# Six words of a hand-written order, each one slice further from the words that feed them, in an attention and two-layer mixture-of-experts kernel

## The chip, the cores and the metric

The kernel runs on one core of a Trainium2 chip, as one program of one launch. The metric is device time in microseconds of one execution. The median of three runs before the change is 425.94 us (424.27 to 426.3).

## The reference

Linear attention over 4 batches of 576 tokens and 8 heads of 64, then two mixture-of-experts layers over the 2304 rows of 512 that it gives. Each layer has 8 experts of 512 x 1024 x 512, and a token goes to the one expert with the largest logit.

```python
q_s = softmax(q, over the 64 of a head);  k_s = softmax(k, over the 576 tokens)
kv = np.einsum('bhsd,bhse->bhde', k_s, v)
x = np.einsum('bhsd,bhde->bhse', q_s, kv)        # then reshaped to 2304 x 512

# layer 1: capacity 576 tokens for each expert, counted in order of tokens
logits = x @ w_gate;  expert_idx = argmax(logits);  gate_w = max of softmax(logits)
out[i] = gate_w[i] * (relu(x[i] @ w1[e]) @ w2[e])      # 0 where the expert is full

# layer 2: only tokens with x @ w_skip > 0
out = x + gate_w * (relu(x @ w1b[e]) @ w2b[e])         # else out = x
```

## The kernel before, in words

The tokens lie transposed in memory, 512 features in four pieces of 128 partitions and 576 tokens of a batch in the free dimension. Attention of a batch is done in two halves of four heads (the objects `c` to `i`, class `Half`). Routing of a batch in a layer is a `Route` object: `C0` to `C3` for layer 1, `M0` to `M2` for layer 2. An expert with more than 32 tokens of a batch is a "large" one and is computed for all 576 tokens of the batch at once, with the gate weights set to zero for the tokens of others (class `Group`). An expert with up to 32 tokens is a "small" one: its tokens are gathered first (class `Small`, the objects `S` and `T`).

A group has 16 slices. Slices 0 to 7 are products with the first weights (line 839), slices 8 to 15 with the second (line 860). A slice is 24 matmuls of 288 columns. Each 32-bit operand is split in a high and a low part (lines 781 and 782, on ScalarE and VectorE), and a product is three matmuls: high by high, high by low, low by high. Its result lies in one of two pairs of PSUM banks (`pair`). In slices 0 to 7 ScalarE and VectorE take it out as `hh` and `hl` (lines 873 and 874). The slice after the next writes to the same pair, and so waits for `hl`.

The order of everything after the start is written by hand in the table `COURSE`: five groups of 16 lines each. In line i the program issues the products of slice i, then the split of the weights of slice i + 2 (`split_w`), then the words ahead of the bar, then the evacuation of slice i, then the words behind the bar. Each engine does its own instructions in that order. A word is a step of another piece of work that is placed among the slices. Those that matter here:

- `C0.3`, `M0.3`, `M1.3` (`w3`, line 621): VectorE makes the one-hot table `oh` of the chosen expert, a chain of small instructions that ends in line 632 or, in layer 2, in line 636.
- `C0.4`, `M0.4`, `M1.4` (`w4`, line 638): 17 small TensorE matmuls in 16 bits on `oh` count positions and tokens of each expert in the bank `pp` (lines 644, 652, 660 and 669). VectorE then copies `pos` and `cnt` out (lines 674 to 678).
- `C0.5`, `M0.5`, `M1.5` (`w5`, line 680): VectorE makes the list of large and small experts from `cnt`, some 15 to 20 instructions of one to eight columns.
- `g.rw`, `i.rw` (line 507): for batch 3 the gate weights of layer 1 are multiplied into k v. TensorE turns the product of k and v (`kvd`) in the bank `pkT`, ScalarE copies it as `kT` (line 513), TensorE multiplies with the gate weights (`pkw`, line 517), VectorE copies the result `kw` out (line 520).
- `i.kz` (line 413): VectorE adds k's exponentials over the tokens of a partition in three instructions (lines 417 to 419). `i.kv` then turns these sums on TensorE (line 426) and multiplies k and v (line 437).
- `d.km` (line 374): VectorE takes maxima of k in three instructions (lines 378 to 380). `d.kt` turns them on TensorE (line 386). `c.qt` turns q (lines 463 and 470), `c.qn` and `c.q3` normalise q and take exponentials (lines 362 to 367, and 334).

Of the kernel before, what the change touches and what calls it, by code (L numbers as in the profile page):

```python
# [45 lines left out]
    L4 c.qm | C0.1 c.km  # L46
    c.q1 | c.kt
    L5 c.q2 | C0.2 c.kc
    C0.3 c.ke d.qm | C0.4
    L6 C0.5 c.q3 | c.kv  # L50
    c.qn d.q1 |
    L7 d.km | c.qt d.kt
    C0.6 d.q2 | d.kc
    d.ke | c.re G.0
# [26 lines left out]
    ((0, 2), """  # L81
    L4 C2.5 | M0.1
    C2.6 | M0.2
    L5 G.3 S.p M0.3 | S.g0 M0.4
    M0.5 | S.g1 G.1
    L6 M0.6 S.l | S.g2
    | S.g3 G.2
    L7 | S.g4
# [9 lines left out]
    """),  # L98
    ((1, 0), """
    L4 G.3 | g.rw  # L100
    | M2.1
    L5 | M2.2 M1.1
    M2.3 | M2.4
    L6 M2.5 | G.1
    M2.6 | M1.2
    L7 T.p M1.3 T.l G.2 | T.g0 M1.4
    M1.5 | T.g1
    M1.6 N0 | T.g2
    X0 i.qm | T.g3
    N1 i.km i.q1 | T.g4 i.kt  # L110
    X1 i.q2 | T.gx i.kc
    N2 i.ke | T.t00 O0.0
    X2 i.kz i.q3 | i.kv
    N3 i.qn | T.t01 O0.1
    X3 T.v0 | T.t02 i.qt
    """),
    ((1, 1), """
    L4 G.3 | T.t03 O0.2
    | T.a0 i.rw
    L5 | T.t04 C3.1  # L120
    T.v1 | T.t10 T.u00
    L6 | T.u01 C3.2 G.1
    C3.3 | T.t11 C3.4 O0.3
# [15 lines left out]
def kernel(  # L139
# [18 lines left out]
    B, H, S, D = q.shape  # L158
    DM = out.shape[1]
    E = w_gate.shape[1]  # L160
# [21 lines left out]
    def bank(name):  # L182
        return pa.tile([P, 512], F32, name=name, tag="a")
# [39 lines left out]
    wg = []  # L223
    for i, g in enumerate((w_gate, w_gate2)):
        t = cp.tile([P, NC, 32], F32, name=f"wg{i}")
        nc.gpsimd.memset(t, 0.0)
        with nc.allow_non_contiguous_dma(reason="gate weights are small"):
            nc.scalar.dma_start(out=t[:, :, 0:E], in_=g.rearrange("(c p) e -> p c e", p=P))
            if i == 1:
                nc.scalar.dma_start(  # L230
                    out=t[:, :, E:E + 1], in_=w_skip.rearrange("(c p o) -> p c o", p=P, o=1)
# [33 lines left out]
    class Half:  # L265
# [241 lines left out]
        def rw(self):  # L507

            kT = self.tile([P, 2, P], "kT", "m2")
            pt = bank("pkT")  # L510
            for c in range(2):
                nc.tensor.transpose(pt[:, c * P:(c + 1) * P], self.kd[:, c], ident)
            nc.scalar.copy(kT, pt[:, :2 * P].rearrange("p (c t) -> p c t", c=2))
            pt = bank("pkw")
            o = 2 * self.hh
            for c in range(2):
                nc.tensor.matmul(
                    out=pt[:, c * E:(c + 1) * E], lhsT=kT[:, c], rhs=wg[0][:, o + c, 0:E], start=True, stop=True
                )
            nc.vector.tensor_copy(out=kw[:, o:o + 2, 0:E], in_=pt[:, :2 * E].rearrange("p (c e) -> p c e", c=2))  # L520

# [956 lines left out]
```

## Time and profile before

| | |
|---|---|
| median of three runs | 425.94 us (424.27, 425.94, 426.3) |
| the profiled execution | 423.36 us; span of its instructions 421.5 us |
| TensorE (PE) busy in the span | 396.1 us, 94% |
| weight loads (PEld) | 351.3 us, 83% |
| VectorE (DVE) | 251.8 us, 60% |
| ScalarE (ACT) | 182.5 us, 43% |
| GpSimd (POOL) | 12.3 us, 3% |
| DMA | 54.48 MB, mean 129 GB/s |
| mean granted clock of TensorE | 0.994 |

The profile is of one execution, whose time lies 2.58 us below the median. A matmul of the large groups overlaps with the next, so a row's duration is longer than its distance to the next row. "[1.10 <-DVE oh L636]" behind a row says that the engine stood idle for 1.10 us ahead of it, and what ended that.

### The profile page before, as it was taken

Reading aid. Unit: us, or ns where it says so; the run is one execution under the profiler, and the core shown is the slowest. Engines: PE = TensorE matmul, PEld = TensorE weight load, DVE = VectorE, ACT = ScalarE, POOL = GpSimd, SP = SyncE. Lnnn points to the kernel's source line nnn. Section 1 sums busy time; section 2 is a strip of 40 time slices with the busy share of each in tenths; the row PEclk is TensorE's granted clock in tenths of the full one; section 3 lists DMA queues with packets and bytes.
Section 4 is the critical chain, followed back from the end, with each engine's and each line's share of the span. In section 5 each row is a group of like instructions: output and inputs, shape, how many; then the busy total and the mean of one; then the engine's idle time right before and its main releaser. Section 6 shows DMA issues by size and latency. Waiting matters only on the chain.

```text
span 421.5 us, 8456 instructions
## 1 busy us (share of the span) xinstructions
PE 396.1 (94%) x3241; PEld 351.3 (83%) x3241; DVE 251.8 (60%) x640; ACT 182.5 (43%) x547; POOL 12.3 (3%) x46
## 2 busy tenths in 40 slices
PE   8989879999999999998999999998999999899893
PEld 4656779898999889798999888798998987799882
DVE  3875788463686755378446746367676736554431
ACT  1556666634257771423347523332375333231111
POOL 2400000000000000000000100000000000000000
PEclk9999999999999999999999999999999999999997
DMA  8819935200960300392544861117315555363134
GB/s 199 221 51 255 235 93 163 58 2 2 310 159 25 106 2 2 111 291 68 163 166 151 241 180 51 50 52 231 98 51 180 178 178 174 92 212 145 30 90 110
DMA packets 72536, 54.48 MB, mean 129 GB/s; under 512 B 18455, under 2 KB 67115, under 8 KB 72491
## 3 DMA queue, kind: packets, MB, share of 16 engines
q1 hardware_dynamic: 70536, 53.60, 44.1%
q10 hardware_dynamic: 1954, 0.31, 0.5%
q8 instruction: 26, 0.43, 0.4%
q14 instruction: 20, 0.16, 0.1%
HBM read 49.16 MB, written 4.73 MB: 128 GB/s over the span
## 4 chain that ended last, share of the span: by engine, by line
PE 70%; DVE 6%; ACT 3%; issue 2%; DVEq 0%; ACTq 0%
PE pair L860 29%; PE pair L839 21%; PE pxs L1147 2%; PE pk L437 2%; PE pl L593 2%; PE pto L1281 2%; PE ph L1203 1%; PE py L1203 1%; PE pts L1252 1%; PE px L495 1%; ACT hh L873 1%; PE ptq L463 1%; DVE wl L782 1%; PE ptx L1162 1%; DVE hl L874 1%
## 5 line engine op out<-in xcount | busy, mean ns | idle before, releaser
L860 PE MATMUL pair<-hh,wh 128*128 128x288 f32 x320 | 98.2, 307 | 0.0
L860 PE MATMUL pair<-hh,wl 128*128 128x288 f32 x320 | 94.4, 295 | 0.0
L860 PE MATMUL pair<-hl,wh 128*128 128x288 f32 x320 | 94.4, 295 | 0.0
L839 PE MATMUL pair<-xh,wh 128*128 128x288 f32 x304 | 92.9, 305 | 0.0
L839 PE MATMUL pair<-xl,wh 128*128 128x288 f32 x304 | 89.6, 295 | 0.0
L839 PE MATMUL pair<-xh,wl 128*128 128x288 f32 x304 | 89.4, 294 | 0.0
L782 DVE TENSOR_TENSOR wl<-ws,wh 128x512 fp32r<-128x512 f32 x80 | 54.9, 686 | 36.4 <-ACT wh L781 34.8
L873 ACT ACTIVATE hh<-pair 128x576 fp32r<-128x576 f32 x40 | 25.9, 647 | 88.6 <-PE pair L839 86.8
L860 PEld LDWEIGHTS pair<-hh,wh 128*128 128x128 f32 x320 | 60.4, 189 | 3.8 <-issue 2.6
L860 PEld LDWEIGHTS pair<-hl,wh 128*128 128x128 f32 x320 | 60.6, 189 | 0.1
L860 PEld LDWEIGHTS pair<-hh,wl 128*128 128x128 f32 x320 | 60.4, 189 | 0.0
L839 PEld LDWEIGHTS pair<-xh,wh 128*128 128x128 f32 x304 | 57.0, 188 | 2.3 <-issue 0.9
L874 DVE SCALAR_TENSOR_TENSOR hl<-pair,hh 128x576 fp32r<-128x576 f32 x40 | 30.2, 756 | 46.4 <-ACT hh L873 46.4
L839 PEld LDWEIGHTS pair<-xl,wh 128*128 128x128 f32 x304 | 57.1, 188 | 0.1
L839 PEld LDWEIGHTS pair<-xh,wl 128*128 128x128 f32 x304 | 57.1, 188 | 0.0
L781 ACT CAST wh<-ws 128x512 fp32r<-128x512 f32 x80 | 49.3, 620 | 2.6 <-DMA ws<-in_moe_w_dram 1.7
L334 ACT ACTIVATE eq<-qt,mx 128x64 f32<-128x64 f32 x140 | 46.7, 338 | 0.3 <-DVE mx L323 0.3
L334 ACT ACTIVATION_READ_ACCUMULATOR eq<-qt,mx 128x1 f32 x140 | 26.6, 190 | 0.0
L532 PE MATMUL pair<-warm 128*128 128x384 f16 x94 | 19.7, 359 | 1.6 <-DVE warm L949 1.6
L782 DVE TENSOR_TENSOR xl<-x,xh 128x576 fp32r<-128x576 f32 x20 | 14.9, 752 | 6.0 <-ACT xh L781 6.0
L1282 ACT COPY ot<-pto 128x256 f32<-128x256 f32 (+1 forms) x24 | 7.0, 316 | 26.0 <-PE pto L1281 26.0
L532 PEld LDWEIGHTS <-warm 128*128 128x128 f16 x94 | 9.6, 107 | 8.8 <-issue 3.2
(210 smaller groups left out, 499.9 us busy)
## 6 DMA issues: line engine op xcount, KB each, us to landing
ws<-in_moe_w_dram SPq DMA_DIRECT2D x39, 512.0 KB, 5.4
tw<-in_moe_w_dram SPq DMA_DIRECT2D x24, 512.0 KB, 4.1
kt<-in_k_dram SPq DMA_DIRECT2D x8, 512.0 KB, 7.7
qt<-in_q_dram SPq DMA_DIRECT2D x8, 512.0 KB, 6.8
out_dram<-ot SPq DMA_DIRECT2D x12, 256.0 KB, 2.7
vt<-in_v_dram SPq DMA_DIRECT2D x16, 128.0 KB, 4.5
vt<-in_v_dram SPq DMA_DIRECT2D x3, 512.0 KB
mg<-gate SPq DMA_DIRECT2D x4, 288.0 KB, 6.1
```

The lines of the kernel that those rows point to most:

```text
L334: nc.scalar.activation(self.eqv[:, h, j], self.qt[:, h, j], AF.Exp, bias=self.mx[:, i:i + 1], accum_out=self.qz[:, i:i + 1])
L437: nc.tensor.matmul(out=pk[64 * g:64 * g + 64, c * D1 + o:c * D1 + o + n], lhsT=self.kt[:rows(j), 2 * c + g, j], rhs=ones32[:rows(j), 0:1] ...
L532: nc.tensor.matmul(out=pw[:, 0, :3 * P], lhsT=warm16[:, 0:P], rhs=warm16, start=True, stop=True)
L593: nc.tensor.matmul(out=pl[32 * c:32 * c + 32, :HT], lhsT=self.weights[:, c], rhs=self.chunk(c, tokens(a)), start=True, stop=True,)
L781: nc.scalar.copy(hi, src)
L782: nc.vector.tensor_tensor(out=lo, in0=src, in1=hi.bitcast(F32), op=ALU.subtract)
L839: nc.tensor.matmul(out=self.pt[:, a, :HT], lhsT=u[:, c], rhs=w[:, c, tokens(a)], start=(c == 0 and n == 0), stop=(c == NC - 1 and n == 2),)
L860: nc.tensor.matmul(out=self.pt[:, a, :HT], lhsT=p_[:, f], rhs=w[:, tokens(a)], start=(v == 0 and f == 0 and n == 0), stop=(v == 1 and f == ...
L873: nc.scalar.activation(halves(hh), src, AF.Relu)
L874: nc.vector.scalar_tensor_tensor(out=halves(hl), in0=src, scalar=0.0, in1=halves(hh).bitcast(F32), op0=ALU.max, op1=ALU.subtract,)
L1147: nc.tensor.matmul(out=self.px[:, c * self.w:(c + 1) * self.w], lhsT=self.xt[:rows(j), c * P:(c + 1) * P], rhs=self.pj[:rows(j), j], start ...
L1203: nc.tensor.matmul(out=self.ph[32 * g:32 * g + 32, :256], lhsT=lhsT, rhs=rhs, start=(i % 4 == 0), stop=(i % 4 == 3))
```

## The change

Six words are moved by one place, and `rw` is cut in two so that its second half can stand apart:

- `C0.4` from behind the bar of slice 3 to ahead of the bar of slice 4 in the first group, `C0.5` from slice 4 to slice 5;
- `M0.4` and `M1.4` in the same way (slices 2 to 3 of the third group, 6 to 7 of the fourth), with `M0.5` and `M1.5` from ahead of the bar to behind it;
- `g.rw` and `i.rw` keep the turn and the copy `kT`; the matmuls `pkw` and the copy `kw` are the new words `g.rx` and `i.rx`, one slice later;
- `i.kz` from ahead of the bar of slice 13 of the fourth group to behind the bar of slice 12.

```diff
-    C0.3 c.ke d.qm | C0.4
-    L6 C0.5 c.q3 | c.kv
-    c.qn d.q1 |
+    C0.3 c.ke d.qm |
+    L6 C0.4 c.q3 | c.kv
+    C0.5 c.qn d.q1 |
...
-    L4 G.3 | g.rw
-    | M2.1
+    g.rx | M2.1
...
-    N2 i.ke | T.t00 O0.0
-    X2 i.kz i.q3 | i.kv
+    N2 i.ke | T.t00 O0.0 i.kz
+    X2 i.q3 | i.kv
...
             nc.scalar.copy(kT, pt[:, :2 * P].rearrange("p (c t) -> p c t", c=2))
+            self.kT = kT
+
+        def rx(self):
             pt = bank("pkw")
```

On VectorE, in slices 3 to 5 of the first group (`hl` is the evacuation of a slice, `wl` the low part of the weights, `pos` and `cnt` belong to C0.4, `keep` begins C0.5), before:

```order
L874 SCALAR_TENSOR_TENSOR hl<-pair_83,hh 128x576
L674 COPY pos<-pp 128x40
L676 TENSOR_TENSOR cnt<-pp,rem 128x8
L782 TENSOR_TENSOR wl_208<-ws_201,wh_204 128x512
L685 TENSOR_TENSOR keep<-pos,rem 128x40
```

and with the change:

```order
L877 SCALAR_TENSOR_TENSOR hl<-pair_83,hh 128x576
L785 TENSOR_TENSOR wl_208<-ws_201,wh_204 128x512
L677 COPY pos<-pp 128x40
L679 TENSOR_TENSOR cnt<-pp,rem 128x8
L877 SCALAR_TENSOR_TENSOR hl<-pair_84,hh 128x576
L454 TENSOR_SCALAR rz<-pk 128x2
L455 RECIPROCAL rz<-rz 128x2
L458 TENSOR_TENSOR kvd_113<-pk,rz 64x2x64 x2
L785 TENSOR_TENSOR wl_209<-ws_201,wh_205 128x512
L688 TENSOR_TENSOR keep<-pos,rem 128x40
```

The two copies now stand behind a split of weights and ahead of the next slice's `hl`, and C0.5 stands behind that `hl` and the four rows that follow it. What stands behind C0.5 (`c.qn`, then an `hl`, a `wl` and `d.km`) keeps its place.

On VectorE, in slices 12 and 13 of the fourth group (`s` is i.kz, `ot` a copy of a store, `xl` the low part of the next group's input), before:

```order
L1282 COPY ot<-pto 128x256
L782 TENSOR_TENSOR wl_209<-ws_201,wh_205 128x512
L782 TENSOR_TENSOR xl<-x_122,xh 128x576
L417 TENSOR_TENSOR s_3878<-kt 128x512
L418 TENSOR_TENSOR s_3879<-s_3878 128x256
L419 TENSOR_TENSOR s_3879<-s_3879,kt 128x256
```

and with the change:

```order
L1285 COPY ot<-pto 128x256
L417 TENSOR_TENSOR s_3850<-kt 128x512
L418 TENSOR_TENSOR s_3851<-s_3850 128x256
L419 TENSOR_TENSOR s_3851<-s_3851,kt 128x256
L785 TENSOR_TENSOR wl_209<-ws_201,wh_205 128x512
L785 TENSOR_TENSOR xl<-x_122,xh 128x576
```

The three sums pass the two splits.

On TensorE, at slices 0 and 1 of the fourth group, before:

```order
L839 MATMUL pair_84<-xh,wl_206 128x288
L512 MATMUL pkT<-c_85,kvd_113 128x128 x2
L517 MATMUL pkw<-wg_93,kT 128x8 x2
L839 MATMUL pair_83<-xh,wh_203 128x288
L839 MATMUL pair_83<-xl,wh_203 128x288
```

and with the change, at the turn and then at the end of slice 1:

```order
L512 MATMUL pkT<-c_85,kvd_113 128x128 x2
L842 MATMUL pair_83<-xh,wh_203 128x288
L842 MATMUL pair_83<-xl,wh_203 128x288
```

```order
L842 MATMUL pair_83<-xh,wl_207 128x288
L520 MATMUL pkw<-wg_93,kT 128x8 x2
L596 MATMUL pl<-x_123,wg_96 32x288 x8
```

The 24 matmuls of slice 1 now stand between `pkT` and `pkw`. The matmuls of `pp` pass the 24 of the next slice in the same way at their three places. No instruction is added or taken away, and the orders of ScalarE, GpSimd and the DMA queue are as before.

## Rows read from the trace of the kernel before

**Rows 1.** Waits of TensorE: engine, line, releaser: us in total, times, longest.
```profile
PE pp L644 <- DVE oh L636: 2.2, 2, 1.1
```
**Rows 2.** Timeline of TensorE around C0.4: start, us, engine, line, operation [idle before].
```profile
58.72 0.27 PE L644 MATMUL pp<-oh,c 128*128 128x32 f16 x4 [2.12 <-DVE oh L632]
...
59.48 0.40 PE L839 MATMUL pair<-xh,wh 128*128 128x288 f32 x1
...
62.87 1.83 PE L437 MATMUL pk<-vt,kt 128*64 128x65 f32 x40
...
72.39 0.38 PE L386 MATMUL pt<-c,m 128*128 128x128 f32 x2
```
**Rows 3.** Timeline of TensorE at M0.4 (third group) and M1.4 (fourth group).
```profile
197.45 0.27 PE L644 MATMUL pp<-oh,c 128*128 128x32 f16 x4 [1.10 <-DVE oh L636]
...
290.42 0.26 PE L644 MATMUL pp<-oh,c 128*128 128x32 f16 x4 [1.13 <-DVE oh L636]
```
**Rows 4.** Timeline of TensorE at g.rw (fourth group) and i.rw (fifth group).
```profile
262.49 0.38 PE L512 MATMUL pkT<-c,kvd 128*128 128x128 f32 x2
263.65 0.61 PE L517 MATMUL pkw<-wg,kT 128*128 128x8 f32 x4 [0.79 <-ACT kT L513]
264.12 0.38 PE L839 MATMUL pair<-xh,wh 128*128 128x288 f32 x1
...
344.71 0.61 PE L517 MATMUL pkw<-wg,kT 128*128 128x8 f32 x4 [0.60 <-ACT kT L513]
```
**Rows 5.** Timeline of TensorE at i.kz and i.kv, slice 13 of the fourth group.
```profile
323.11 0.41 PE L426 MATMUL pt<-c,s 128*128 128x128 f32 x2 [0.70 <-DVE s L419]
```
**Rows 6.** Timeline of TensorE where a slice follows a turn without a wait.
```profile
206.88 0.63 PE L1162 MATMUL ptx<-c,x 128*128 128x128 f32 x4
207.27 0.38 PE L839 MATMUL pair<-xh,wh 128*128 128x288 f32 x1
```
**Rows 7.** Timeline of VectorE before C0.4: what slice 4 of the first group needs.
```profile
52.52 0.68 DVE L782 TENSOR_TENSOR wl<-ws,wh 128x512 fp32r<-128x512 f32 x1
...
54.42 0.76 DVE L874 SCALAR_TENSOR_TENSOR hl<-pair,hh 128x576 fp32r<-128x576 f32 x1 [1.22 <-ACT hh L873]
```
**Rows 8.** Timeline of VectorE from C0.4 to d.km, slices 3 to 6 of the first group.
```profile
60.84 0.19 DVE L674 COPY pos<-pp 128x40 f32<-128x40 f32 x1
...
61.02 0.69 DVE L782 TENSOR_TENSOR wl<-ws,wh 128x512 fp32r<-128x512 f32 x1
61.62 0.19 DVE L685 TENSOR_TENSOR keep<-pos,rem 128x40 f32<-128x40 f32 x1
...
68.80 0.76 DVE L874 SCALAR_TENSOR_TENSOR hl<-pair,hh 128x576 fp32r<-128x576 f32 x1 [0.34 <-ACT hh L873]
...
71.31 0.43 DVE L380 TENSOR_TENSOR m<-m,kt 128x256 f32<-128x256 f32 x1
```
**Rows 9.** Timeline of ScalarE, slice 4 of the first group: c.q3, next evacuation.
```profile
61.23 0.19 ACT L334 ACTIVATION_READ_ACCUMULATOR eq<-qt,mx 128x1 f32 x1
62.97 0.65 ACT L873 ACTIVATE hh<-pair 128x576 fp32r<-128x576 f32 x1 [1.56 <-PE pair L839]
```
**Rows 10.** Timeline of the weight loads of TensorE at C0.4.
```profile
58.72 0.17 PEld L644 LDWEIGHTS <-c 128*128 128x128 f16 x4 [2.35 <-DVE oh L632]
```
**Rows 11.** Timeline of VectorE at M0.4.
```profile
198.32 0.20 DVE L674 COPY pos<-pp 128x40 f32<-128x40 f32 x1 [0.26 <-PE pp L669]
...
198.51 0.68 DVE L782 TENSOR_TENSOR wl<-ws,wh 128x512 fp32r<-128x512 f32 x1
```
**Rows 12.** Timeline of the DMA queue of SyncE: the load that waits for M1.5's list.
```profile
293.70 0.38 SPq L799 DMA_DIRECT2D ws<-in_moe_w_dram  x1
```
**Rows 13.** Timeline of VectorE: the split that first reads that load.
```profile
325.95 0.69 DVE L782 TENSOR_TENSOR wl<-ws,wh 128x512 fp32r<-128x512 f32 x1
```

More of the change, by code (lines that the diff above doesn't have):

```diff
@@ L83 @@
     C2.6 | M0.2
-    L5 G.3 S.p M0.3 | S.g0 M0.4
-    M0.5 | S.g1 G.1
+    L5 G.3 S.p M0.3 | S.g0
+    M0.4 | M0.5 S.g1 G.1
     L6 M0.6 S.l | S.g2
@@ L105 @@
     M2.6 | M1.2
-    L7 T.p M1.3 T.l G.2 | T.g0 M1.4
-    M1.5 | T.g1
+    L7 T.p M1.3 T.l G.2 | T.g0
+    M1.4 | M1.5 T.g1
     M1.6 N0 | T.g2
@@ L119 @@
     | T.a0 i.rw
-    L5 | T.t04 C3.1
+    L5 i.rx | T.t04 C3.1
     T.v1 | T.t10 T.u00
@@ L517, in rw @@
                 nc.tensor.matmul(
-                    out=pt[:, c * E:(c + 1) * E], lhsT=kT[:, c], rhs=wg[0][:, o + c, 0:E], start=True, stop=True
+                    out=pt[:, c * E:(c + 1) * E], lhsT=self.kT[:, c], rhs=wg[0][:, o + c, 0:E], start=True, stop=True
                 )
```

## The prediction

> **What bounds the kernel now.** I read the page first: TensorE is busy for 94% of the span and VectorE for 60%, so time is won where TensorE stands still. The waits of TensorE then tell on whom. The reader is to see that it waits twice, 2.2 us in all, for the one-hot table of layer 2 [rows 1]: the counts stand right behind the words that make the table. The timeline of TensorE then shows that all six moved words have such a wait: 2.12 us ahead of C0.4 [rows 2], 1.10 ahead of M0.4 and 1.13 ahead of M1.4 [rows 3], 0.79 at g.rw and 0.60 at i.rw [rows 4], 0.70 at i.kv, which waits for i.kz [rows 5]. That is 6.44 us. Last I read VectorE's timeline behind each place, since VectorE is what made TensorE late there.
>
> **What a wait costs beside its length.** Without a wait, a matmul starts before the listed end of the one ahead: the turn ptx ends at 206.88 + 0.63 = 207.51, and the slice starts at 207.27, so 0.24 us overlap [rows 6]. With a wait this overlap is lost, and the weight loads show why: they too stood idle, for 2.35 us where the matmuls stood for 2.12, though they load a constant [rows 10]. So I add 0.24 us to each of the four places behind a turn (M0.4, M1.4, g.rw, i.rw) and 0.1 at i.kv, taken between nothing and 0.24 since a full slice is ahead of it: 1.06 us in all. The Trainium skill, page "TensorE: Matmul & The Clock Gate", section "Part 2: What happens when you issue a matmul", says that TensorE's queue draws weight loads ahead of running matmuls. By that the load would be done during the wait, the 1.06 us would not exist, and the time would be 421.1; the row on the weight loads speaks against it here.
>
> **The change part by part.** Nothing is added or removed, so the price of each move is where its work lands. On ScalarE, GpSimd and SyncE the order stays, so nothing is moved past on their queues; only what they wait for can come later.
>
> C0.4, the largest wait, is mostly not won. TensorE can start slice 4 at 58.72 - 2.12 = 56.60: its weights were split by 52.52 + 0.68 = 53.20, its banks were free at 54.42 + 0.76 = 55.18 [rows 7]. Its 24 matmuls take 62.87 - 59.48 = 3.39 us [rows 2], the counts 59.48 - 58.72 = 0.76 [rows 2], so pp is full at 60.75. VectorE, however, works from 60.84 without a gap until 68.80 - 0.34 = 68.46 and then stands 0.34 us [rows 8]. It does the same instructions after the change, in another order, up to the last maximum of d.km, which ends at 71.31 + 0.43 = 71.74 and which d.kt's turn on TensorE needs. From 60.84 on: the split of weights first, 61.62 - 61.02 = 0.60, then the two copies, 61.02 - 60.84 = 0.18 [rows 8], so it is at 61.62 when it comes to slice 4's hl. That needs ScalarE's hh, which stands behind c.q3's exponentials until 61.23 + 0.19 = 61.42 and takes 0.65 [rows 9]: about 62.0 to 62.1. So VectorE gets a new gap of some 0.4 us, and loses the old one of 0.34, because slice 5 now ends earlier. d.km ends at about 71.8, and the turn starts at about 71.9 instead of 72.39 [rows 2]. TensorE, 2.36 us ahead by then, would be there at 70.0 and waits some 1.8 us in a new place. Won: 0.5 us; bounds 0 and 2.36 (2.12 + 0.24).
>
> M0.4 and M1.4. VectorE is not full here: it waited 0.26 us for pp itself [rows 11]. The copies now wait longer, and hl behind them is late by the copies, some 0.3 us; the slice that needs its banks comes a whole slice later. M0.5 and M1.5 come later too. M1.5's list feeds the load of the next group's weights, which SyncE issued at 293.70 [rows 12]; 2 us of delay there lie under the 32 us until the first split reads it at 325.95 [rows 13]. The same holds for the gate of G.1, whose copy stands behind M0.5 on VectorE: its time is set by a turn on TensorE behind the same slice, and the gate is read only in the second half of the group. Won: 1.10 + 1.13, and 0.48 of overlap; bounds 2.23 and 2.71.
>
> g.rw and i.rw. pkT is followed by a slice at once; pkw costs the same 264.12 - 263.65 = 0.47 us [rows 4] a slice later, when kT has long been copied. kw is read by C3.1, after a whole slice for g and, for i, after the 16 matmuls of T.t04. Won: 0.79 + 0.60, and 0.48 of overlap; bounds 1.39 and 1.87.
>
> i.kz. The three sums go ahead of the two splits, which nobody waits for within the slice. i.kv's turn finds them done. Won: 0.70 and 0.1; bounds 0.70 and 0.94.
>
> **The sum.** 0.5 + 2.23 + 1.39 + 0.70 = 4.82, with the overlap 1.06: 5.9 us. The profiled execution takes 423.36 us (span 421.5), so 417.5 for it. It lies 2.58 us under the median of the runs, so I take the sum off the median: 425.94 - 5.9 = **420.0 us**. With the bounds 4.3 and 7.9 (0 + 2.23 + 1.39 + 0.70; 2.36 + 2.71 + 1.87 + 0.94) it is 418.0 to 421.6. The three runs spread by 1 us to either side.
>
> **The rivals.** 1. *The whole wait at C0.4 comes back.* VectorE would have to be free for d.km at 70.0. For it: it has a gap of 0.34 us. Against it: only that one. The Trainium skill, the same page, section "Part 1: The HAM clock gate", under the architectural detail, calls VectorE's queue a strict FIFO. By that rule d.km can't pass C0.5, and this rival is out; the trace agrees, as a split behind the waiting copy starts only after it [rows 11]. Time: all upper bounds, 418.0.
>
> 2. *VectorE gives part of it back at M0.4 and M1.4.* The copies now hold up hl until pp is full; where the next slice but one finds its banks taken, some 1.3 us of either place go. For it: two of the four groups' worth of evacuations now stand behind a wait on TensorE. Against it: some 3 us of slack, as a slice takes 3.39 us. Time: 425.94 - (5.9 - 2.6) = 422.6.
>
> 3. *It changes nothing.* Every wait turns up again at the next meeting of the engines, as most of C0.4's does; then 425.9. Against it: behind the five other places no row shows VectorE full.
>
> 4. *Slower, by C0.4 alone.* If slice 4 can't start at 56.60, its matmuls stay at 59.48, pp is full at 62.87 + 0.76 = 63.63, and VectorE, which comes to the copies at 61.44 (60.84 + 0.60), stands before them for 2.2 us, with the whole queue to d.km behind it, and for up to 0.9 more at rz, which reads k v from the bank that TensorE fills after pp. d.km then ends at about 71.74 + 2.2 + 0.9 = 74.8 and TensorE loses 2.5 us at d.kt. If the other slices don't start early for the same reason, nothing stands against it: 428.4. The point is a start of slice 4 at 57.3 (57.3 + 3.39 + 0.76 = 61.45, where VectorE comes to the copies), and from 57.8 on the place costs time. Against it: both things that I see slice 4 wait for are there by 55.18 [rows 7].
>
> That the change doesn't do what it says is no rival: the rows of the order show each move.
>
> **How the numbers follow.** Forecast 0.62, rival 1 0.10, rival 2 0.14, rival 3 0.10, rival 4 0.04. A difference from the median of over 0.5%, 2.13 us, is what a measurement of this kernel can tell: the limits are 423.8 and 428.1. Forecast and rivals 1 and 2 lie below 423.8: faster 0.86. Rival 3 is the same, 0.10; rival 4 slower, 0.04. The range goes from 417.6 (rival 1 and some of the spread of the runs) to 423.2 (rival 2 with as much), and leaves out rivals 3 and 4 and the edges.
>
> **What the profile of the changed kernel would show.** No idle time ahead of pp's first matmuls in the first, third and fourth group, none ahead of pkw, none ahead of the turn of the sums s. In its place a new wait of 1.5 to 2.0 us of d.kt's turn for d.km's last maximum, in slice 6 of the first group; VectorE idle some 1.5 us ahead of M0.4's and M1.4's copies. Up to d.kt the profile should be ahead by 0.5 us, at the end of the third group's slice 3 by 1.8, at the end by 5.9. I would be wrong if the new wait is missing or is longer than 2.36 us, or if slices 5 of the third and 9 of the fourth group wait for an evacuation.

## The result, and the profile after

| | before | after |
|---|---|---|
| median | 425.11 us (4 runs, 423.6 to 426.3) | 417.46 us (4 runs, 416.55 to 418.01) |
| profiled execution, span | 423.36, 421.5 us | 416.55, 414.7 us |
| TensorE busy | 396.1 us | 393.7 us |
| mean granted clock of TensorE | 0.994 | 0.995 |

The ratio is 0.984, interval 0.9815 to 0.9864: 7.65 us faster. The forecast was 5.9 us faster, at 420.0, and the time lies 0.14 us below the low end of the range. The sign and the places were right; below I show that the sum came out within 0.2 us between two executions that start alike, and that it was taken off the wrong number.

TensorE's waits after the change, with the releaser, us in total, times and longest. The lines for pp [rows 1] and for pkw are gone. The turn of d.kt has a longest wait of 1.6 us, and q's turn a new one of 0.2:

```profile
PE pt L386 <- DVE m L380: 3.4, 4, 1.6
...
PE ptq L470 <- DVE eq L367: 0.2, 1, 0.2
```

TensorE's timeline after the change, at the six places in order of time. Compare [rows 2 to 5]: no row of pp, of pkw or of the turn of s has a wait behind it any more.

```profile
58.79 0.27 PE L647 MATMUL pp<-oh,c 128*128 128x32 f16 x4
...
71.13 0.41 PE L386 MATMUL pt<-c,m 128*128 128x128 f32 x2 [1.64 <-DVE m L380]
...
197.95 0.27 PE L647 MATMUL pp<-oh,c 128*128 128x32 f16 x4
...
263.22 0.51 PE L520 MATMUL pkw<-wg,kT 128*128 128x8 f32 x4
...
288.49 0.27 PE L647 MATMUL pp<-oh,c 128*128 128x32 f16 x4
...
317.15 0.38 PE L426 MATMUL pt<-c,s 128*128 128x128 f32 x2
...
341.14 0.51 PE L520 MATMUL pkw<-wg,kT 128*128 128x8 f32 x4
```

VectorE's timeline after the change, first at C0.4 and d.km, then at M0.4 (compare [rows 8, 11]):

```profile
60.02 0.68 DVE L785 TENSOR_TENSOR wl<-ws,wh 128x512 fp32r<-128x512 f32 x1
60.62 0.19 DVE L677 COPY pos<-pp 128x40 f32<-128x40 f32 x1
...
61.16 0.76 DVE L877 SCALAR_TENSOR_TENSOR hl<-pair,hh 128x576 fp32r<-128x576 f32 x1 [0.28 <-ACT hh L876]
...
68.05 0.76 DVE L877 SCALAR_TENSOR_TENSOR hl<-pair,hh 128x576 fp32r<-128x576 f32 x1
...
70.56 0.43 DVE L380 TENSOR_TENSOR m<-m,kt 128x256 f32<-128x256 f32 x1
...
198.82 0.20 DVE L677 COPY pos<-pp 128x40 f32<-128x40 f32 x1 [1.57 <-PE pp L672]
...
199.01 0.75 DVE L877 SCALAR_TENSOR_TENSOR hl<-pair,hh 128x576 fp32r<-128x576 f32 x1
```

At C0.4 VectorE runs from the split to d.km's last maximum with one gap of 0.28 us ahead of slice 4's hl, and the old gap ahead of slice 5's hl, 0.34 us [rows 8], is gone. So d.km ends when VectorE's own work allows it, and TensorE waits for it. At M0.4 VectorE stands 1.57 us ahead of the copies and then goes on; no slice behind it waits for an evacuation.

**Start-up differs between executions**, so the two profiles can't be laid on each other from zero. The same turn, ahead of every moved word, in the profile before and in that after:

```profile
13.42 0.67 PE L398 MATMUL pmax<-dm,ones 128*128 128x256 f32 x2 [0.51 <-DVE capf L248]
```

```profile
12.60 0.67 PE L398 MATMUL pmax<-dm,ones 128*128 128x256 f32 x2 [0.65 <-DVE capf L248]
```

The profile after is 0.82 us ahead before it comes to the change. A second profile of the changed kernel, taken with the experiments, starts within 0.03 us of the one before:

```profile
13.45 0.67 PE L398 MATMUL pmax<-dm,ones 128*128 128x256 f32 x2 [0.51 <-DVE capf L248]
```

It took 417.53 us, and 423.36 - 417.53 = **5.83 us** is the effect between two like executions. The forecast, 5.9 off the profiled execution, was 417.5.

The lead place by place, as the difference of the starts of one matmul behind each place, against the profile before. The first column is that matmul's start before, the next two its start in the two profiles of the changed kernel. The term of the forecast stands with its share of overlap.

| behind | before | after | after, second | gained (second) | forecast |
|---|---|---|---|---|---|
| start-up (pmax) | 13.42 | 12.60 | 13.45 | -0.03 | |
| C0.4 (pg of G.0) | 81.77 | 80.37 | 81.24 | 0.56 | 0.5 |
| M0.4 (ptx) | 202.32 | 199.63 | 200.51 | 1.28 | 1.34 |
| g.rw (pl) | 267.47 | 263.66 | 264.55 | 1.11 | 1.03 |
| M1.4 (ptx) | 295.31 | 290.20 | 291.08 | 1.31 | 1.37 |
| i.kz (turn of s) | 323.11 | 317.15 | 318.04 | 0.84 | 0.8 |
| i.rw (py) | 348.52 | 341.58 | 342.46 | 0.99 | 0.84 |

The six gains make 6.09 us. At TensorE's last matmul the lead is 6.03 (it starts at 414.94 before and at 408.91 in the second profile), and 0.2 more are lost behind it, in the end of the program, which makes the 5.83. What is left to explain is why the medians differ by 7.65.

### The profile page after: what moved, and what is told of

The parts are those of the page before. It is cut to its first block, busy times and chain, and to the rows that moved or that the text cites. A ratio compares the mean times of both kernels' runs of the same rounds, so it can differ in the third digit from the quotient of the medians.

```text
span 414.7 us, 8456 instructions
## 1 busy us (share of the span) xinstructions
PE 393.7 (95%) x3241; PEld 351.1 (85%) x3241; DVE 251.6 (61%) x640; ACT 182.3 (44%) x547; POOL 12.4 (3%) x46
## 4 chain that ended last, share of the span: by engine, by line
PE 85%; DVE 8%; ACT 3%; issue 2%; DVEq 0%; ACTq 0%
PE pair L863 31%; PE pair L842 25%; PE pair L535 3%; PE px L495 3%; PE pxs L1150 2%; PE pk L437 2%; PE pl L596 2%; PE pto L1284 2%; PE ph L1206 1%; PE py L1206 1%; PE pts L1255 1%; PE pk L992 1%; PE ptq L463 1%; DVE hl L877 1%; PE pair L822 1%
## 5 line engine op out<-in xcount | busy, mean ns | idle before, releaser
L535 PE MATMUL pair<-warm 128*128 128x384 f16 x94 | 18.7, 346 | 1.6 <-DVE warm L952 1.6
```

Of the source, the lines that this page charges most:

```text
L535: nc.tensor.matmul(out=pw[:, 0, :3 * P], lhsT=warm16[:, 0:P], rhs=warm16, start=True, stop=True)
```

## The experiments

**1. The parts by themselves.** Four kernels make a part of the change each. C0.4 and C0.5 alone is this hunk, and the second kernel is everything but it:

```diff
-    C0.3 c.ke d.qm | C0.4
-    L6 C0.5 c.q3 | c.kv
-    c.qn d.q1 |
+    C0.3 c.ke d.qm |
+    L6 C0.4 c.q3 | c.kv
+    C0.5 c.qn d.q1 |
```

The third has M0.4, M0.5, M1.4 and M1.5 alone, the fourth the cut of `rw` and `i.kz` alone. What was expected, in this order:

> C0.4 and C0.5 one place later, everything else as before. Theory (VectorE's queue up to d.km decides): the wait of 2.1 us ahead of pp goes, a new one of 1.5 to 1.8 us stands ahead of d.kt's turn, TensorE is ahead by 0.6 us from there on, and the time is 0.6 us (0.15%) under the kernel before. Rival 1 (the whole wait comes back): 2.1 to 2.4 us, 0.5%. Rival 4 (VectorE's copies hold its queue up): slower by up to 2.5 us.

> The whole change but for C0.4 and C0.5, which stand as before. Theory (the places add up, each with its wait and the lost overlap): the other five give 1.28 + 1.12 + 1.30 + 0.85 + 0.98 = 5.5 us, so 5.5 us (1.3%) under the kernel before, and the pp wait of 2.1 us is there. Rival (the measured 7.65 us hold something beside the places): over 6.5 us.

> M0.4, M0.5, M1.4 and M1.5 alone. Theory: 1.28 + 1.30 = 2.6 us (0.6%) under the kernel before, which is more than the two waits of 1.10 and 1.13 by the overlap that a wait loses; no slice waits for an evacuation behind it. If the overlap is no part of the gain: 2.2 us. Rival 2 (hl behind the copies holds the banks up): 1.3 us or less, and a wait of the matmuls of slice 5 of the third group or 9 of the fourth.

> g.rx, i.rx and i.kz alone. Theory: 1.12 + 0.98 + 0.85 = 2.95 us (0.7%) under the kernel before, against 2.1 us of waits. If the overlap is no part of the gain: 2.1 us. Rival (the wait of pkw turns up at C3.1, which reads kw): under 2 us, and a wait of the matmuls pl in the fifth group.

Measured, beside 22 runs of the kernel before with a median of 424.04 us (423.03 to 425.98):

| | median, us | ratio, interval | gained | gained at its places in the trace |
|---|---|---|---|---|
| C0.4 alone | 422.34 (12 runs) | 0.9952 (0.9936 to 0.9968) | 1.70 | 0.56 |
| all but C0.4 | 418.63 (6 runs) | 0.9863 (0.9836 to 0.9889) | 5.41 | 5.52 |
| M0.4 and M1.4 alone | 421.67 (7 runs) | 0.9939 (0.9917 to 0.9962) | 2.37 | 2.57 |
| rw and kz alone | 422.04 (6 runs) | 0.9943 (0.9916 to 0.997) | 2.00 | 2.96 |

The last column is worked out as in the table above. Each place gives in its own kernel what it gives in the whole change, within 0.03 us (M0.4 1.25 and 1.26, M1.4 1.30 and 1.31, g.rw 1.14 and 1.12, i.kz 0.85 and 0.86, i.rw 0.98 twice): the places don't touch each other. Two of the times don't follow, though: C0.4 alone gives 1.1 us more than its place, rw and kz 0.96 less.

**The clock.** The profile of the kernel with M0.4 and M1.4 alone shows the first reason. It still has C0.4's wait, 2.14 us, and its lead of 0.57 us from the start turns into a lag of 0.98 between C0.4 and the product of k and v behind slice 4. Its stretches around that wait (us; length, TensorE busy and matmuls; granted clock, DMA share, GB/s):

```profile
56.00:58.00 2.00, 0.03 (x1) 1.00 0.00 0
58.00:60.00 2.00, 1.82 (x24) 0.96 0.82 214
60.00:62.00 2.00, 2.00 (x11) 0.50 0.20 56
62.00:64.00 2.00, 2.00 (x14) 0.69 0.00 0
```

Behind the wait and the counts that follow it the granted clock falls to 0.50, that is from 2.4 to 1.2 GHz, and only 11 matmuls go through a stretch that takes 17 to 18 elsewhere. Two matmuls of slice 4 in that kernel, each with the one behind it, first at the upper and then at the lower level: 0.13 us from start to start, and then 0.24:

```profile
59.32 0.29 PE L842 MATMUL pair<-xh,wl 128*128 128x288 f32 x1
59.45 0.29 PE L842 MATMUL pair<-xh,wh 128*128 128x288 f32 x1
...
60.31 0.44 PE L842 MATMUL pair<-xh,wl 128*128 128x288 f32 x1
60.55 0.44 PE L842 MATMUL pair<-xh,wh 128*128 128x288 f32 x1
```

In these 6 us TensorE lost 0.08 + 1.0 + 0.62 = 1.7 us of its upper clock, and its place against the profile before went back by 0.57 + 0.98 = 1.55 us. The kernel with rw and kz alone has the same at its M1.4 wait of 1.13 us, and falls from a lead of 0.63 to a lag of 0.88 there:

```profile
288.00:290.00 2.00, 0.87 (x15) 1.00 0.87 305
290.00:292.00 2.00, 2.00 (x22) 0.70 0.97 391
292.00:294.00 2.00, 2.00 (x10) 0.50 0.16 59
294.00:296.00 2.00, 2.00 (x18) 0.95 0.76 262
```

No such stretch is in the profiles before and after: there the granted clock is 1.00 until TensorE has nothing left to do. The profile before, behind its waits at C0.4 and at M1.4:

```profile
58.00:60.00 2.00, 1.28 (x21) 1.00 0.50 123
60.00:62.00 2.00, 2.00 (x18) 1.00 0.49 147
...
292.00:294.00 2.00, 2.00 (x17) 1.00 0.29 109
```

Other executions of the kernel before have a lower mean clock, though none of them was profiled. All the 55 runs of the kernel before that were made beside the experiments, by their mean granted clock:

| mean granted clock | runs | us | median |
|---|---|---|---|
| 0.993 or 0.994 | 29 | 423.03 to 424.16 | 423.54 |
| 0.990 or 0.991 | 18 | 423.84 to 424.78 | 424.24 |
| 0.983 to 0.989 | 8 | 425.87 to 427.07 | 425.99 |

The mean also counts the end of the span, where TensorE has nothing left to do: in the profile before the granted clock is 0.50 for the last 5.4 us, in that of the kernel with two filled waits (experiment 2) for the last 3.0. By that end alone the means would be 0.994 and 0.996 (estimates: half of it, over the span), which is what the two runs have. A fall that costs 1.7 us of the upper clock takes off another 0.004. So 0.990 and 0.986 fit one and two falls, and 0.997 against 0.994 is no sign of a fall; but the sort isn't exact, since a run at 0.993 could have a fall and a short end.

All 9 runs of the changed kernel are at 0.995 to 0.997 (median 417.23), and all 12 with C0.4 alone at 0.993 or 0.994. Five of the six with rw and kz alone are at 0.992 or below, and the sixth, at 0.994, took 420.8, which is 2.6 us under 423.43, the median of the ten runs before at 0.993 or 0.994 that were made beside it.

**2. The wait kept, TensorE kept busy.** If the lower clock follows the waits, the kernel before should lose its spread when TensorE has something to do in them, though nothing starts earlier. In `w4` of the kernel before:

```diff
             ppv = pp[:, :NJ * E].rearrange("p (j e) -> p j e", j=NJ)
+            if self.s == (0, 0):
+                for _ in range(18):
+                    nc.tensor.transpose(pp[:, 0:P], ident, ident)
```

> The kernel before, with 18 turns of a constant on TensorE into the bank pp ahead of C0.4's first matmul: TensorE is busy for most of the 2.12 us for which it waited, and C0.4's matmuls start when they did, at 58.7. Theory (what makes executions of the kernel before differ is the granted clock falling to 1.2 GHz after this wait): no run of this kernel at a mean clock of 0.985 or 0.986, nearly all at 0.993 or above as in the kernel with C0.4 alone moved, median 423.4 (that of the 10 runs of the kernel before at 0.993 and 0.994), and spread below 1.5 us instead of 3. Rival (clock and time vary for another reason, the start or a later place): clocks and times as in the kernel before, median 424.0, spread 3 us. If the turns take longer than the wait they add up to 0.3 us to either.

The wait is filled, and C0.4 begins as it did relative to the slice ahead. TensorE's timeline of this kernel:

```profile
55.72 2.13 PE L645 MATMUL pp<-c 128*128 128x128 f32 x18
58.01 0.25 PE L647 MATMUL pp<-oh,c 128*128 128x32 f16 x4 [0.16 <-DVE oh L632]
```

Measured: 423.97 us (12 runs, 422.81 to 424.32), ratio 0.9993 (0.9978 to 1.0007). Half of it came: the spread is 1.5 us and no run is below 0.990, where 5 of the 39 runs before until then were at 0.986 or less. The median missed: 7 of the 12 runs are at 0.990 or 0.991. The profile, one of them, says where, at M1.4's wait, which was not filled:

```profile
288.00:290.00 2.00, 0.87 (x16) 1.00 0.90 309
290.00:292.00 2.00, 2.00 (x22) 0.90 0.89 344
292.00:294.00 2.00, 2.00 (x10) 0.50 0.12 45
294.00:296.00 2.00, 2.00 (x14) 0.74 0.87 261
```

So a second kernel of this kind fills that one too, with 10 turns:

```diff
-            if self.s == (0, 0):
-                for _ in range(18):
+            if self.s in ((0, 0), (1, 1)):
+                for _ in range(18 if self.m == 0 else 10):
```

> The kernel before, with 18 turns of a constant ahead of C0.4's first matmul as in the kernel with filler at C0.4 alone, and 10 such turns ahead of M1.4's, so that TensorE is busy for about 1.1 of the 1.13 us that it waits there. Nothing starts earlier by it. Theory (the lower clock follows these two waits): the two groups of that kernel's runs, 0.990 and 0.991 at 424.1 us and 0.993 to 0.997 at 422.8 to 423.8, become one; all runs at 0.993 or above, median 423.4, spread below 1.2 us, and no stretch of the profile at a lower clock before the end. Rival (the clock falls for a reason that has nothing to do with these waits): about half the runs at 0.991 or below again, median 424.0.

Measured: **423.10 us** (12 runs, 422.41 to 424.15) beside 424.07 of the kernel before, ratio 0.9975 (0.9957 to 0.9993). The kernel to which 28 turns were added has the lower median. 10 of the 12 runs are at 0.993 or above, 2 at 0.990 (424.08 and 424.15), where 26 of the 55 runs before are at 0.991 or below. Its profile has the upper clock through M1.4:

```profile
288.00:290.00 2.00, 1.96 (x27) 1.00 0.99 365
290.00:292.00 2.00, 2.00 (x24) 1.00 0.95 381
292.00:294.00 2.00, 2.00 (x18) 1.00 0.08 29
```

The runs speak for the theory: 2 of 12 are at 0.991 or below, where 8 of the 16 beside them are. They don't settle it. The expectation that all runs would be at 0.993 or above and spread by less than 1.2 us missed (the spread is 1.74), and where the clock fell in the two others no profile shows; M0.4's wait and the shorter ones were not filled. The median came out lower than forecast, too: it is 0.54 us under 423.64, the median of the 8 runs beside it at 0.993 or 0.994, and the falls don't explain that part. In the profile nothing on TensorE but the start is earlier: the lead on the profile before is 0.69 us at pmax, and 0.68 or 0.69 at every matmul of the table above.

**3. The new wait of d.kt.** Can the 1.64 us be had as well? C0.5 goes one slice further, behind d.km on VectorE; a second kernel also takes q's exponentials ahead of C0.6's on ScalarE. Both start from the changed kernel:

```diff
-    C0.5 c.qn d.q1 |
-    L7 d.km | c.qt d.kt
-    C0.6 d.q2 | d.kc
+    c.qn d.q1 |
+    L7 d.km | C0.5 c.qt d.kt
+    d.q2 C0.6 | d.kc
```

The first kernel leaves the last line as `C0.6 d.q2 | d.kc`. The changed kernel ran beside them.

> The changed kernel, and in the first group C0.5 one slice later still, behind d.km and slice 6's evacuation on VectorE. Theory (VectorE's queue up to d.km decides when d.kt can turn): the new 1.64 us wait of d.kt for its maximum is gone, and the 0.22 us wait of q's turn for eq with it, since c.qn also stands ahead of C0.5 now; TensorE starts d.kt's turn at about 69.3 instead of 71.13. But C0.5's 2.6 us now stand ahead of the step that makes dm from the turned maxima, and C0.6's exponentials on ScalarE come later ahead of d.q2: TensorE waits there instead, and I expect most of the 1.9 us to be given back by 80 us: 417.2, between 416.5 and 417.9. Rival (nothing stands behind VectorE any more): the whole 1.9 us stay, 415.6. Rival (two waits for one): slower than the changed kernel, above 418.3.

> As the kernel with C0.5 behind d.km, and d.q2 ahead of C0.6 as well, so that the exponentials of q do not stand behind C0.6's on ScalarE. If what gives the time back in that kernel is ScalarE's order (C0.6's exponentials ahead of q's), this one keeps about 1.5 us: 416.0, between 415.5 and 416.6, and slice 8's product with the gate (pg) starts 1.5 us before the 80.37 of the changed kernel. If it is VectorE's C0.5 ahead of dm, the time is that of the other, 417.2.

> The changed kernel once more, beside the others on one chip: 417.4 (the 4 runs so far lie between 416.55 and 418.01), all at a mean granted clock of 0.995 or above if the wait at C0.4 is what lets the clock fall.

Measured, beside 423.84 us of the kernel before: the first **417.37** (6 runs, 416.54 to 419.33; ratio 0.9847, 0.9822 to 0.9872), the second **415.50** (5 runs, 414.76 to 416.0; ratio 0.9794, 0.9772 to 0.9816), the changed kernel 417.15 (5 runs, 416.69 to 417.53; ratio 0.9834, 0.9812 to 0.9856). TensorE's timeline of the first:

```profile
70.00 0.38 PE L386 MATMUL pt<-c,m 128*128 128x128 f32 x2
73.85 0.67 PE L398 MATMUL pmax<-dm,ones 128*128 128x256 f32 x2 [0.29 <-DVE dm L392]
...
79.79 0.66 PE L489 MATMUL px<-qT,kvd 128*128 128x64 f32 x4 [0.38 <-DVE kt L404]
81.62 2.55 PE L936 MATMUL pg<-c,gm 128*128 128x128 f32 x10 [1.17 <-ACT x L502]
```

and of the second:

```profile
70.28 0.38 PE L386 MATMUL pt<-c,m 128*128 128x128 f32 x2
74.14 0.67 PE L398 MATMUL pmax<-dm,ones 128*128 128x256 f32 x2 [0.29 <-DVE dm L392]
...
79.53 0.55 PE L489 MATMUL px<-qT,kvd 128*128 128x64 f32 x4
79.95 1.52 PE L936 MATMUL pg<-c,gm 128*128 128x128 f32 x10
```

In both the wait of d.kt is gone: VectorE's queue up to d.km was what set it. In the first the time comes back as 0.29 + 0.38 + 1.17 us of other waits, the last for ScalarE's copy of `x`. ScalarE's timeline in the first and in the second, the exponential of C0.6 (`ex`) and the copy `x`:

```profile
74.45 0.24 ACT L744 ACTIVATE ex<-ex 128x40 f32<-128x40 f32 x1 [3.09 <-DVE ex L743]
...
81.00 1.05 ACT L502 COPY x<-px 128x512 f32<-128x512 f32 x2
```

```profile
74.74 0.24 ACT L744 ACTIVATE ex<-ex 128x40 f32<-128x40 f32 x1 [0.77 <-DVE ex L743]
...
79.33 1.06 ACT L502 COPY x<-px 128x512 f32<-128x512 f32 x2
```

In the first ScalarE stands 3.09 us for `ex`, with q's seven exponentials and the evacuation behind it. In the second these come ahead and `x` is copied 1.67 us earlier, so pg starts 1.29 us earlier than in the second profile of the changed kernel (81.24), from a start-up 0.36 us later (pmax at 13.81, against 13.45). Two of the six runs of the first, at 0.990 and 0.991, took 419.2 and 419.3 us, the others 416.54 to 417.41. The profile is one of the two: behind pg's new wait its clock falls as well:

```profile
80.00:82.00 2.00, 0.83 (x6) 0.95 0.02 4
82.00:84.00 2.00, 2.00 (x10) 0.50 0.00 0
84.00:86.00 2.00, 2.00 (x11) 0.70 0.00 0
```

The second version is 1.65 us under the changed kernel on the same chip, and its slowest run (416.0) is faster than the fastest of the changed kernel (416.69). That is at the low end of what was expected of it (415.5 to 416.6).

## Why the prediction was right, and where not

- **C0.4** (0.5 us, with a new wait of 1.5 to 2.0 at d.kt): 0.56 by the trace, and the wait is 1.64. The gap moved as argued, 0.28 us where 0.4 was put. Rival 1 is out: TensorE met VectorE again at d.kt. Rival 4 is out: slice 4 started at once, and pp waited for nothing.
- **M0.4 and M1.4** (2.71 with overlap): 2.59. VectorE stands 1.57 us ahead of the copies where "some 1.5" was forecast, and nobody waits for the hl behind them, which puts rival 2 out.
- **g.rw, i.rw, i.kz** (2.67): 2.94. Rival 3 is out: none of these waits turned up again.
- **The overlap**, 1.06 us, was there. The five places gained 1.28, 1.31, 1.11, 0.99 and 0.84 where their waits were 1.10, 1.13, 0.79, 0.60 and 0.70 [rows 3 to 5]: 1.21 us beyond the waits. What the weight loads have to do with it is argued and not shown by itself, and the prediction read one of them wrongly. At M0.4, as at C0.4 [rows 10], the load is of a constant, and it stood idle with the matmul, 1.34 us where the matmul stood 1.10. At g.rw and i.rw the weights of `pkw` are `kT`, the very tile that TensorE waited for:

```profile
197.45 0.16 PEld L644 LDWEIGHTS <-c 128*128 128x128 f16 x4 [1.34 <-DVE oh L636]
...
263.65 0.52 PEld L517 LDWEIGHTS pkw<-wg,kT 128*128 128x128 f32 x4 [1.02 <-ACT kT L513]
```

The Trainium skill's rule that weight loads are drawn ahead of running matmuls (page "TensorE: Matmul & The Clock Gate", section "Part 2: What happens when you issue a matmul") therefore says nothing of these two places, and the 421.1 that the prediction gave by it should have been 420.6 (an estimate, with their 0.48 left in). At M0.4 the trace doesn't show the load drawn ahead: for a matmul that is itself waiting, the measurement decides.
- **The step that failed is the number from which the sum was taken**: "so I take the sum off the median". The sum itself, 5.9 us off the profiled execution, came out at 5.83 between like starts; that it fits so closely is in part luck, as the places make 6.09, with M0.4 and M1.4 0.12 below their forecast and the other three 0.27 above. The 2.58 us between the profiled execution and the median were taken to stay as they are, and they did not. By their times, two of the three runs behind that median, 425.94 and 426.3, are of the kind that had a mean clock of 0.989 or below among the 55, and only 8 of the 55 are: two of three was bad luck. The median of all 55 is 424.02. That the falls of the kernel before lie behind its waits at C0.4 and M1.4, which the change takes away, is read from profiles of kernels that keep these waits (experiments 1 and 2); none of the kernel before itself shows one. The runs of the kernel before at 0.993 or 0.994 have a median of 423.54, the changed kernel 417.23 over its 9 runs: 6.31 us, of which some tenths beyond 5.83 stay open. The rest of the 7.65 is that the four runs shown hold those two. Had the sum been taken off the profiled execution, with its clock of 1.00 up to the end, the forecast would have been 417.5.
- For C0.4 alone the same reason covers about half of what is beyond its place, 0.6 of 1.14 us: against the runs before at 0.993 or 0.994 made beside it, it gains 1.1 instead of 1.70. Between two profiles of like start it gains 423.36 - 422.65 = 0.71. Between that and 0.56 at its place, and between 0.71 and 1.1, some tenths stay open.

## What to carry over

A moved word was worth the wait ahead of it plus the overlap that the wait destroyed, as long as the engine that made it late had room behind; where that engine was full, as VectorE up to d.km, the wait turned up at its next hand-over, and moving the work that fills the queue is the next step. Before a sum is taken off a median, sort the runs by their granted clock: a sum from a trace belongs to runs that look like the traced one, and a wait may have a second price that the trace of one execution doesn't show. Where such a wait can't be removed, idle turns in it may already be worth something: two waits filled with 28 of them gave 0.25% here (0.07 to 0.43%), about half of which the falls of the clock don't explain.

## What the runs showed of the hardware

The granted clock went to 1.2 GHz behind waits of TensorE of 2.14 us and of 1.13 us in a stream that was else busy, and behind a third of 1.17 us in an experiment; it cost 1.7 us of the upper clock each time. It does not do so each time: the profile before has both waits at a clock of 1.00, and by the mean clock 29 of the 55 runs of that kernel are like it. Nor does the length of a wait alone decide it here. The changed kernel's own wait of 1.64 us at d.kt has no run below 0.995 among 9. In the kernel with C0.4 alone, which has that wait and keeps M1.4's of 1.13 us, no run of 12 was below 0.993, while the kernel with C0.4's wait filled, which keeps the same wait at M1.4, had 7 of 12 at 0.990 or 0.991; why is open. So is why the runs of the kernel before at 0.990 or 0.991 are only 0.70 us above the others, when a fall set TensorE back by some 1.5: the profiles with a fall also began at other times, between 7.41 and 8.69 us for the first turn of d.kt's kind, but with one profile a kernel nothing can be made of it.
